# The lead of an attention-and-MLP kernel: projection tiles in groups of four, two begun on either half of the array's rows

## The chip, the cores and the metric

The kernel runs on one core of a Trainium2 chip. The metric is the device time of one execution in microseconds (us). Engines are named as in the profile: PE is TensorE (matmuls), PEld its weight loads, DVE is VectorE, ACT is ScalarE, POOL is GpSimd, SP is SyncE, which here issues all the DMAs (its queue is SPq). "L305" is line 305 of the kernel.

## What is computed

```
xn  = layernorm(x)                       # x: 2048 rows, 512 wide, f32
qkv = xn @ wqkv                          # 32 heads of 16
p   = softmax(q @ k.T * 16 ** -0.5)      # per head, 2048 x 2048
s   = (p @ v) @ wo
h   = relu(xn @ w1 + b1) ** 2            # 1792 wide
out = x + s * silu(h @ w2 + b2)
```

## The kernel before

**Halves of the array.** Every f32 operand of a projection is split into a high and a low part, and a product takes three matmuls (high by high, high by low, low by high). Most matmuls use 64 of the 128 rows, rows 0 to 63 (lane 0) or 64 to 127 (lane 1), and one of each lane can run at the same time. PE takes its instructions strictly in the written order, so the order says which two stand side by side.

**Three kinds of small work.** A max (max_mm, L305 with its reduction on DVE, L313) takes 128 x 512 scores of one head and keeps their row maximum; there are 2048 of them, 1024 per lane, in three rotating PSUM banks pm. After 64 maxes of a unit u (4 heads by 512 queries) the shift is worked out on DVE and sent through DRAM into rows of the tile qe. An exp (exp_mm, L1283, then ACT at L1289) is a score block whose exponential goes to a tile pt; its matmul writes one of three banks se. A PV step (L379) multiplies four pt tiles with v into the bank po.

**The full tiles.** After the layernorm 16 projection tiles of 128 x 512 are made with all 128 rows (q_tile, L991, 12 matmuls each), among the transposes of the layernorm and behind them. They make k and q of the first heads and most of v. Their results go to DRAM (k_d, q_d, v_d) and come back as ka (keys) and qm (queries for the maxes).

**The lead.** Then come 31 projection tiles in halves (lead_halves, L1040, 12 matmuls on lane 0 and 12 on lane 1 into one bank), with maxes in between. Lane 0 takes tile after tile; lane 1 does the same tiles 23 places later (`far = [None] * (15 + LAG)`). Before lane 1 may touch a bank, a dependency makes it wait for a later max of lane 0. At the start the list far is empty but for a few maxes, and at the end what is left in far runs beside eight maxes of lane 0. Each tile ends in q_end: ACT copies the bank to raw (L1020, two buffers), POOL splits it into hl (L82 and L83, three buffers), and SP stores hl (q_d or k_d). Beside the tiles stand, by a counter b, loads and stores for later: the transposed input to DRAM (xn_d, 1 MB each), the keys of the next heads, v, the queries qe.

**The loop.** After it, blocks ("slots") of one key block each: 512 slots with exps, maxes, matmuls of the MLP (L207 in halves, L239 in blocks of both lanes) and a PV step two slots behind. Slots 0 and 1 carry four exps and four maxes each and, by pump(6), the last projection tile, made with all 128 rows (L991 into pd). Slots 2 and 3 have no MLP matmuls. Slot 4 begins the MLP: it needs the first 256 columns of the input, xc, in four DMAs by quarters of the contraction, and the first weights w1s, which come as ex and are split by POOL. A planner (long_slots, ahead_m) chooses between two shapes of a slot pair by the number of maxes done so far.

PE, and in the first part ACT, DVE and POOL, run in the order of the program text; SP's order in the lead is left to the scheduler.

## Time and profile before

| what | us |
|---|---|
| median of 3 runs (1638.95 to 1640.37) | 1639.32 |
| the profiled execution | 1642.99 |
| its span from first to last instruction | 1641.1 |
| PE busy / DVE busy / ACT busy / POOL busy | 1621.3 / 1350.6 / 1181.7 / 516.4 |
| first matmul of the lead | 64.48 |
| first matmul of slot 2 | 189.81 |

Times inside the trace count from the start of the span. The mean granted TensorE clock over the span is 0.996. In rows of the timeline the columns are start, length, engine, line, operation, output and inputs, and in brackets the idle time just before and what ended it. In rows of windows each engine's busy time is followed by the number of its instructions, and then by the granted clock.

### The profile page before, as it was taken

What the parts mean: (1) busy time and instruction counts of PE and PEld (TensorE: products, weight loads), DVE (VectorE), ACT (ScalarE), POOL (GpSimd) and SP (SyncE); (2) the same over time, 40 slices, a digit from 0 to 9 for tenths busy, and PEclk for the clock granted to TensorE, in tenths of its full rate; (3) what the DMA queues carried; (4) which work ended last, traced back from release to release, by engine and by line L of the source; (5) the groups of instructions that cost most, each with busy time, mean ns of one, the idle gap of its engine ahead of it and who ended that gap; (6) DMA issues with size and microseconds to landing.
All of it is one profiled execution on the core that took longest, in us unless ns stands there. A gap on an engine that the chain in (4) does not pass through costs nothing.

```text
span 1641.1 us, 35386 instructions
## 1 busy us (share of the span) xinstructions
PE 1621.3 (99%) x13627; PEld 979.2 (60%) x13627; DVE 1350.6 (82%) x2335; ACT 1181.7 (72%) x2339; POOL 516.4 (31%) x541
## 2 busy tenths in 40 slices
PE   7999999999999999999999999999999999999998
PEld 6799666556656655565566556645665565454455
DVE  6399988887788888888888888888888888888843
ACT  6221477778878877787777777877877777777785
POOL 5335567513211321222123103311331133213224
PEclk9899999999999999999999999999999999999999
DMA  8596555426232522342333423343341442415444
GB/s 304 158 270 222 180 177 163 130 54 170 86 87 83 162 72 81 102 128 70 93 99 111 114 71 111 95 107 82 112 121 50 105 142 62 105 48 171 122 147 143
DMA packets 150465, 201.44 MB, mean 123 GB/s; under 512 B 50008, under 2 KB 67416, under 8 KB 148760
## 3 DMA queue, kind: packets, MB, share of 16 engines
q1 hardware_dynamic: 150296, 199.17, 41.6%
q8 instruction: 108, 1.77, 0.5%
q14 instruction: 61, 0.50, 0.1%
HBM read 144.84 MB, written 53.99 MB: 121 GB/s over the span
## 4 chain that ended last, share of the span: by engine, by line
PE 94%; DVE 2%; issue 2%; DMA 1%; POOL 0%; SPq 0%; ACT 0%; DVEq 0%
PE po L379 30%; PE pm_t L305 17%; PE pd_t L239 17%; PE se L1283 15%; PE pd_t L207 5%; PE se L1040 3%; PE pd_t L787 2%; DVE mx L313 2%; PE pd_t L1040 1%; PE po L1040 1%; PE se L991 1%; DMA ka<-k_d 1%; PE pm_t L1283 0%; DMA xt<-in_A_x_dram 0%; POOL wr_t L944 0%
## 5 line engine op out<-in xcount | busy, mean ns | idle before, releaser
L313 DVE TENSOR_REDUCE mx<-pm_t 128x1 f32<-128x512 f32 x2048 | 1267.9, 683 | 208.7 <-PE pm_t L305 123.1
L1289 ACT ACTIVATE pt<-se 128x512 f32<-128x512 f32 x1738 | 924.0, 615 | 227.3 <-PE se L1283 156.5
L305 PE MATMUL pm_t<-ka,qm 64*128 64x512 f32 x2048 | 784.5, 418 | 4.2 <-DVE mx L313 2.4
L1283 PE MATMUL se<-qe,ka 64*128 64x512 f32 x2009 | 735.0, 413 | 0.4 <-DMA qe<-sh_d 0.2
L379 PE MATMUL po<-pt,v 128*32 128x512 f32 x3554 | 526.6, 602 | 0.0
L305 PEld LDWEIGHTS pm_t<-ka,qm 64*128 64x128 f32 x2048 | 360.6, 185 | 219.5 <-DVE mx L313 205.2
L1283 PEld LDWEIGHTS se<-qe,ka 64*128 64x128 f32 x2009 | 350.5, 184 | 103.1 <-ACT pt L1289 61.8
L239 PEld LDWEIGHTS pd_t<-xc,w1s 64*128 64x128 f32 x2352 | 295.7, 187 | 47.3 <-issue 45.3
L239 PE MATMUL pd_t<-xc,w1s 64*128 64x256 f32 x2352 | 322.0, 286 | 0.0
L239 PE MATMUL pd_t<-w2t,hT 64*128 64x512 f32 x936 | 253.2, 406 | 0.0
L379 PE MATMUL po<-ex,v 128*32 128x512 f32 x542 | 226.5, 602 | 0.0
L1289 ACT ACTIVATE ex<-se 128x512 f32<-128x512 f32 x271 | 163.4, 616 | 42.1 <-PE se L1283 30.2
L239 PEld LDWEIGHTS pd_t<-w2t,hT 64*128 64x128 f32 x936 | 159.5, 184 | 48.5 <-issue 40.2
L379 PEld LDWEIGHTS po<-pt,v 128*32 128x32 f32 x3554 | 88.2, 108 | 154.3 <-issue 141.1
L558 POOL TENSOR_TENSOR r<-r 128x512 f32<-128x512 f32 x49 | 50.9, 1039 | 331.9 <-ACT r L555 331.9
L577 POOL TENSOR_TENSOR u<-u,b_t 128x512 f32<-128x512 f32 x16 | 20.7, 1296 | 365.0 <-ACT u L576 365.0
L207 PE MATMUL pd_t<-w2t,hT 64*128 64x512 f32 x408 | 106.1, 392 | 0.0
L207 PEld LDWEIGHTS pd_t<-w2t,hT 64*128 64x128 f32 x408 | 72.5, 184 | 9.6 <-DVE mx L313 0.7
L787 PE MATMUL pd_t<-wot,oc 64*128 64x512 f32 x267 | 76.9, 406 | 0.0
L417 POOL TENSOR_TENSOR ot<-ot,hl 128x512 f32<-128x512 f32 x31 | 39.8, 1284 | 109.1 <-DMA hl<-r_d 80.9
L83 POOL TENSOR_TENSOR hT<-r,hT 128x512 fp32r<-128x512 f32 x56 | 72.2, 1289 | 4.7
L1040 PE MATMUL se<-xT,wr_t 64*128 64x512 f32 x336 | 71.4, 390 | 0.0
(133 smaller groups left out, 1213.4 us busy)
## 6 DMA issues: line engine op xcount, KB each, us to landing
w1s<-w_d SPq DMA_DIRECT2D x196, 256.0 KB
k_d<-hl SPq DMA_DIRECT2D x32, 256.0 KB
xn_d<-xT SPq DMA_DIRECT2D x8, 1024.0 KB
q_d<-hl SPq DMA_DIRECT2D x16, 512.0 KB
qm<-q_d SPq DMA_DIRECT2D x128, 64.0 KB
qe<-q_d SPq DMA_DIRECT2D x128, 64.0 KB
ka<-k_d SPq DMA_DIRECT2D x32, 256.0 KB
hl<-r_d SPq DMA_DIRECT2D x31, 256.0 KB
```

Source lines behind the costliest of these rows:

```text
L83: (lo or nc.gpsimd).tensor_tensor(dst[1], raw, dst[0].bitcast(F32), op=ALU.subtract)
L207: mm = nc.tensor.matmul(out_, lh(r), rh(r), start=first_ and lane == 0, stop=last_ and lane == 1, skip_group_check=True,)
L239: mm = nc.tensor.matmul(out_, lh(r), rh(r), start=first_ and lane == 0, stop=last_ and lane == 1, skip_group_check=True,)
L305: nc.tensor.matmul(ps, qms[u][p][64 * j : 64 * j + 64, qb * P : (qb + 1) * P], kas[qd, p][64 * j : 64 * j + 64, kc * 512 : (kc + 1) * 512] ...
L313: return nc.vector.tensor_reduce(mxs[u][:, c, kc : kc + 1], ps, axis=AX.X, op=ALU.max)
L379: nc.tensor.matmul(po[32 * j : 32 * j + 32, :], vs[qd][:, (4 * kb + j) * VW : (4 * kb + j) * VW + 32], pts[j], start=(kb == 0), stop=(kb = ...
L417: nc.gpsimd.tensor_tensor(ot, ot, hl[:, 1].bitcast(F32), op=ALU.mult)
L558: nc.gpsimd.tensor_tensor(r, r, r, op=ALU.mult)
L787: inst = nc.tensor.matmul(ps[lane], oc[r, a, n, ts_], wot[r, b, n], start=m == 0 and (lane == 0 or wide), stop=m == kos and (lane == 1 or ...
L1040: inst = nc.tensor.matmul(out_, lh(r), rh(r), start=first_ and lane == 0, stop=last_ and lane == 1, skip_group_check=True,)
L1283: nc.tensor.matmul(se, kas[qd, j // 2][b : b + 64, kb * P : (kb + 1) * P], qes[u][j // 2][b : b + 64, :], start=True, stop=True,)
L1289: return nc.scalar.activation(pts[j], se, AF.Exp, scale=0.25)
```

## The change

**The lead** is now 32 tiles in eight groups of four; each group is two streams that are emitted in turn, one operation of lane 0, one of lane 1. In a group lane 0 begins tiles 0 and 2 and then finishes tiles 1 and 3; lane 1 begins 1 and 3 and finishes 0 and 2. Tiles 0 and 1 are in banks se, tile 2 in pd, tile 3 in po. LEAD_AT says after which matmuls of a stream a max stands: 11 in each stream of 48 matmuls, 10 in the first group.

**The last tile** is the fourth of the last group and no longer stands in slots 0 and 1. The eight exps of slots 0 and 1 stand in the last group, after the sixth of every twelve matmuls of a stream, all eight in one bank se that the group takes for them. The loop begins at slot 2; slots 0 and 1 are gone.

**DMAs.** SP's order in the lead is now that of the program text. The first keys and queries are loaded by halves (four loads of ka, four of qm, and again). The events by b stand at the start of every twelve matmuls of lane 0; memsets of ka move into the events b = 2 and 3, those of qm and qe behind the full tiles.

The core of the diff:

```diff
+LEAD_AT = (
+    (3, 8, 12, 17, 22, 26, 31, 36, 40, 45, 48),
+    (1, 5, 10, 14, 19, 24, 28, 33, 38, 42, 47),
+)
...
-        def lead_halves(kind, m, c):
-            ps = q_bank()
+        def lead_halves(kind, m, c, ps, lane0):
...
-                    start=first_ and lane == 0, stop=last_ and lane == 1,
+                    start=first_ and lane == lane0, stop=last_ and lane != lane0,
...
-        for n in range(8):
-            load_k(0, n)
-        qms[0] = load_q(0, "qm")
...
-        rest += [
-            ("qk", m, c) + ((True,) if (m, c) == (7, 3) else ())
-            for c in range(4) for m in (1, 5, 2, 6, 3, 7)
-        ]
+        first.enter_context(tc.manual_schedule(engines={mybir.EngineType.SP}))
+        qms[0] = []
+        for p in range(2):
+            for n in range(4):
+                load_k(0, 4 * p + n)
+            load_q_pair(0, "qm", p, qms[0])
+        rest += [("qk", m, c) for c in range(4) for m in (1, 5, 2, 6, 3, 7)]
...
-        far = [None] * (15 + LAG)
-
-        def step(near):
-            for mine in near:
-                if mine is not None:
-                    mine()
-                if far and far[0] is not None:
-                    far[0]()
-                del far[:1]
-
-        while len(rest) > 1:
...
-            (low, high), behind = lead_halves(*rest.pop(0))
-            low[6:6] = [lambda: max_mm(0)] * (1 + b % 2)
-            low.append(lambda behind=behind: behind(max_mm(0)))
-            high[4:4] = [lambda: max_mm(1)]
-            high[9:9] = [lambda: max_mm(1)]
-            if b % 2 == 0:
-                high.append(lambda: max_mm(1))
...
-        while far:
-            step([lambda: max_mm(0)] + [None] * 2)
...
+        def lead_group(g):
+            items = [rest.pop(0) for _ in range(4)]
+            pools_ = [(pe, "se"), (pe, "se"), (pd, "pd_t"), (pv, "po")]
+            parts = [
+                lead_halves(*item, pool.tile([P, 512], F32, name=name), n % 2)
+                for n, (item, (pool, name)) in enumerate(zip(items, pools_))
+            ]
+            last = g == groups - 1
+            se = pe.tile([P, 512], F32, name="se") if last else None
+            streams = []
+            for lane in range(2):
+                own, other = parts[lane::2], parts[1 - lane :: 2]
+                mms = own[0][0] + own[1][0] + other[0][1] + other[1][1]
+                at = LEAD_AT[lane][: 10 if g == 0 else 11]
...
+                for i, mm in enumerate(mms):
+                    if lane == 0 and i % 12 == 0:
+                        ops.append(lambda b=4 * g + i // 12, mm=mm: [event(b), mm()])
+                    else:
+                        ops.append(mm)
+                    if i + 1 in at:
...
+                        ops.append(m)
+                    if last and i % 12 == 5:
+                        kb, j = divmod(2 * (i // 12) + lane, 4)
+                        ops.append(
+                            lambda kb=kb, j=j: exp_mm(kb, j, pts.setdefault(kb, {}), False, se)
+                        )
...
+            for pair in zip(*streams):
+                for op in pair:
+                    op()
...
-        for st_ in range(NU * 16):
+        assert not rest
+        qs.close()
+        for st_ in range(2, NU * 16):
             if st_ < done:
                 continue
             begin(st_)
-            if st_ < 2:
-                slot(st_, [], None, 6)
-                shift_due()
-                continue
```

**On PE, at the end of the lead and in front of slot 2** (L991 and L1040 are projection matmuls of before, L1026 of the change; L305 and L308 maxes, L1283 and L1205 exps) the last tile stood between maxes and exps:

```order
L1283 MATMUL se<-qe_735,ka_205 128x512
L991 MATMUL pd_t<-xT_188,wr_t 128x512 x6
L305 MATMUL pm_t<-ka_205,qm_203 128x512
L1283 MATMUL se<-qe_734,ka_204 128x512
L305 MATMUL pm_t<-ka_205,qm_203 128x512
L1283 MATMUL se<-qe_735,ka_205 128x512
```

In the last group of the change the exps stand in pairs, one of each lane, at most two matmuls apart; the fourth pair stands like this, with pd and po the tiles that are being finished:

```order
L1026 MATMUL po<-xT_188,wr_t 128x512
L1205 MATMUL se<-qe_735,ka_205 128x512
L308 MATMUL pm_t<-ka_205,qm_203 128x512
L1026 MATMUL po<-xT_188,wr_t 128x512
L1205 MATMUL se<-qe_735,ka_205 128x512
```

Both exps of a pair write the same bank se.

**On SP, around the first loads of the MLP** (ex is the raw first weight, xc the input's first columns, k_d_64 and q_d_60 the last stores of the projections) the last q_d store stood ahead of ex and xc, and the last two k_d stores a dozen DMAs behind them:

```order
L964 DMA q_d_60<-hl 256x1x512
L451 DMA ex_2519<-in_B_w_dram 128x4x128
L493 DMA xc<-xn_d 128x2x256 x4
L451 DMA ex_2520<-in_B_w_dram 128x4x128
L451 DMA ex_2521<-in_B_w_dram 128x4x128
```

Now three stores stand between ex and xc:

```order
L454 DMA ex_2513<-in_B_w_dram 128x4x128
L970 DMA k_d_64<-hl 128x512 x2
L967 DMA q_d_60<-hl 256x1x512
L496 DMA xc<-xn_d 128x2x256 x4
L454 DMA ex_2514<-in_B_w_dram 128x4x128
L454 DMA ex_2515<-in_B_w_dram 128x4x128
```

The stores wait for POOL's split of the last two tiles, and xc has moved behind them.

More of the change, by code (lines that the diff above doesn't have):

```diff
@@ L32 @@
 SHIFT = 8
-LAG = 8
 NVT = 7
@@ L1059, in lead_halves @@
             return [
-                [lambda mm=mm, lane=lane: emit(mm, lane, lane and mm is mms[0]) for mm in mms]
-                for lane in range(2)
-            ], behind
+                [lambda mm=mm, lane=lane: emit(mm, lane, lane != lane0 and mm is mms[0]) for mm in mms]
+                for lane in (lane0, 1 - lane0)
+            ] + [behind]
         xts = {}
@@ L1237 @@
                 load_q_pair(b // 8, "qe", b % 2, qes.setdefault(b // 8, []))
-            if after_v is None and lead[1] == NT:
+            if after_v is None and lead[1] == NT and not any(
+                kind == "v" or m % 4 == 0 for kind, m, _ in rest
+            ) and b % 4 == 0:
                 after_v = b
```

121 lines of the change are left out of this document (55 added, 66 removed).

## The prediction

> **What bounds the kernel now.** I begin with the page: the busy time of the engines and the chain that ended last.
>
> ```profile
> PE 1621.3 (99%) x13627; PEld 979.2 (60%) x13627; DVE 1350.6 (82%) x2335; ACT 1181.7 (72%) x2339; POOL 516.4 (31%) x541
> PE 94%; DVE 2%; issue 2%; DMA 1%; POOL 0%; SPq 0%; ACT 0%; DVEq 0%
> ```
>
> PE is the bound: 94% of the chain is PE. Its instructions stand in a fixed order, so a microsecond that PE saves in the lead is saved at the end, unless a later wait takes it back. A busy PE is not a full PE, though: with one lane at work it counts as busy too. So next I read PE by stretches (length, busy and count, granted clock, DMA share, GB/s).
>
> ```profile
> 61.17:64.58 3.41, 3.41 (x16) 1.00 1.07 183
> 64.58:68.00 3.42, 2.50 (x13) 1.00 1.03 184
> 68.00:71.41 3.41, 3.41 (x13) 0.50 0.93 304
> 71.41:74.82 3.41, 3.41 (x11) 0.50 0.49 189
> 74.82:78.24 3.42, 3.42 (x18) 0.50 0.00 0
> 78.24:81.65 3.41, 3.41 (x32) 1.00 0.16 57
> 180.64:184.05 3.41, 3.17 (x16) 1.00 0.55 183
> ```
>
> At full clock and on both lanes 3.4 us hold 32 half-array matmuls (78.24). The first stretch of the lead holds 13; after it the granted clock is 0.50 until a stretch with 18 has passed. At the end of the lead a stretch with 16 did not lower it. So here the clock falls after about 3.4 us with 13 half matmuls or fewer, and does not with 16.
>
> Then the timeline of PE at both ends of the lead, and the first row of slot 4 that needs xc:
>
> ```profile
> 64.48 0.96 PE L1040 MATMUL pd_t<-wa_t,xT 64*128 64x512 f32 x3
> 66.36 0.47 PE L305 MATMUL pm_t<-ka,qm 64*128 64x512 f32 x1 [0.92 <-DMA ka<-k_d]
> ...
> 189.81 0.39 PE L305 MATMUL pm_t<-ka,qm 64*128 64x512 f32 x1
> ...
> 196.17 0.40 PE L207 MATMUL pd_t<-xc,w1s 64*128 64x256 f32 x2
> ...
> 197.72 1.06 PE L379 MATMUL po<-pt,v 128*32 128x512 f32 x8
> ```
>
> The lead with slots 0 and 1 takes 64.48 to 189.81, **125.3 us**. Call the start of slot 2 T: the first matmul on xc is at T + 6.4, and the PV step that closes slot 4 at T + 7.9. The pace of the middle is read from ACT's copies of finished tiles:
>
> ```profile
> 79.66 0.60 ACT L1000 ACTIVATE vt<-pd_t 128x512 f32<-128x512 f32 x1 [12.96 <-issue]
> ...
> 144.23 0.60 ACT L1020 ACTIVATE raw<-se 128x512 f32<-128x512 f32 x1 [2.89 <-PE se L1040]
> ...
> 157.68 0.60 ACT L1020 ACTIVATE raw<-se 128x512 f32<-128x512 f32 x1 [2.89 <-PE se L1040]
> ...
> 174.66 0.60 ACT L1020 ACTIVATE raw<-se 128x512 f32<-128x512 f32 x1 [2.65 <-PE se L1040]
> ```
>
> From 144.23 to 157.68 four tiles take 13.45 us; each has 12 matmuls and 2.5 maxes per lane, so these are 58 steps of both lanes: **0.232 us a step**.
>
> **The lead, in steps.** By its table the changed lead has 48 + 10 steps in the first group, 48 + 11 in six groups and 48 + 11 + 4 (exps) in the last: 475, at 0.232 us **110.2 us**. The same work at full pairing would have been 477 steps before; the other 14.6 us there are one lane idle at both ends, the halved clock, the 0.92 us wait for ka, and waits in slots 0 and 1.
>
> The start: do the first keys come in time? Before, they were issued behind a weight load:
>
> ```profile
> 51.21 1.17 SPq L967 DMA_DIRECT2D k_d<-hl  x2
> ...
> 55.69 0.39 SPq L952 DMA_DIRECT2D wv<-in_A_wqkv_dram  x1
> 56.20 0.43 SPq L135 DMA_DIRECT2D ka<-k_d  x1
> ```
>
> Now four ka and four qm loads follow these two stores, and that weight load and some xn_d stores come later. With the landing times below (3.1 us, and 1 us per 256 KB queued) they are there by about 62.5, ahead of 64.48. So PE goes from full tiles to full pairs, and the clock stays up.
>
> **Added wait 1: the exps of a pair share one bank.** The second exp's matmul waits until ACT has read the first; behind it the whole of PE waits, since its order is fixed, and with PE the maxes.
>
> ```profile
> 183.36 0.47 PE L1283 MATMUL se<-qe,ka 64*128 64x512 f32 x1
> ...
> 183.86 1.15 ACT L1289 ACTIVATE pt<-se 128x512 f32<-128x512 f32 x2 [0.25 <-DMA qm<-q_d]
> ```
>
> Matmul to ACT is 0.5 us, ACT 0.6 (1.15 for two), and about 0.1 back: 1.2 us against one step of 0.23, a hole of 0.95, four times: **3.8 us**. The bounds are 2.3 (four times ACT alone) and 6.2 (a raw copy of 0.6 ahead of each exp on ACT). I take 3.8, since only the first and last pair have raw copies near them.
>
> **Other waits of the lead.** DVE gets 22 maxes in a group of 59 steps, 13.7 us.
>
> ```profile
> L313 DVE TENSOR_REDUCE mx<-pm_t 128x1 f32<-128x512 f32 x177 | 110.2, 684 | 18.5 <-PE pm_t L305 15.9 <-PE se L1283 0.9 <-PE pd_t L1040 0.8
> ```
>
> At 110.2 / 177 = 0.62 us each that is 13.7: DVE is just as full as PE, where before it had 5 maxes in 3.36 us. Small waits for a free bank must follow a shift, which adds four small DVE instructions. Before, the 28 tiles between the copies at 79.66 and 174.66 lost 0.8 us against their 406 steps; I take **1.3**, bounds 0 and 5.
>
> So slot 2 begins at 64.5 + 110.2 + 3.8 + 1.3 = 179.8, **10.0 us earlier**.
>
> **Added wait 2: xc behind the last stores.** This is the step that gives most of it back. POOL's time for a tile, and SP's rows at the end of the lead before, with the two arrivals of ex:
>
> ```profile
> 135.92 0.62 POOL L82 TENSOR_SCALAR hl<-raw 128x512 fp32r<-128x512 f32 x1 [3.70 <-DMA q_d<-hl]
> ...
> 137.88 0.62 POOL L82 TENSOR_SCALAR hl<-raw 128x512 fp32r<-128x512 f32 x1
> ```
>
> ```profile
> 185.72 0.53 SPq L964 DMA_DIRECT2D q_d<-hl  x1
> 189.34 0.39 SPq L451 DMA_DIRECT2D ex<-in_B_w_dram  x1
> 189.79 2.03 SPq L493 DMA_DIRECT2D xc<-xn_d  x4
> 191.86 3.35 SPq L451 DMA_DIRECT2D ex<-in_B_w_dram  x3
> ```
>
> ```profile
> 192.41 0.41 POOL L82 TENSOR_SCALAR w1s<-ex 128x256 fp32r<-128x256 f32 x1 [0.40 <-DMA ex<-in_B_w_dram]
> ...
> 197.23 0.41 POOL L82 TENSOR_SCALAR w1s<-ex 128x256 fp32r<-128x256 f32 x1 [2.41 <-DMA ex<-in_B_w_dram]
> ```
>
> Before, xc was issued from T on. Now SP must first pass the stores of the two tiles that end with the lead, and these wait for POOL: the matmuls end at T, ACT's first copy at T + 0.7, and POOL needs 1.96 us a tile, so the last is done at T + 4.7. The q_d store goes out, and xc at T + 5.3 to T + 6.8. An ex took 3.07 us from issue to POOL (189.34 to 192.41); the next, with four xc ahead of it, came 4.8 us later, so a 256 KB transfer takes about 0.96. The quarters of xc land at T + 8.4, 9.3, 10.3 and 11.2, or up to 1 us later behind the q_d store's 512 KB. PE wants the first at T + 6.4. With the last quarter's matmuls slot 4 closes at about T + 11.7 and not T + 7.9: **+3.8**, bounds 1.5 (each quarter alone lands in 2 us and the holes are filled by the exps between) and 5. Behind the waiting matmul stand exps, maxes and PV steps, so nothing covers it. The later weights have their slack: the second ex lands near T + 12.5, for slot 6 at about T + 15.6.
>
> **The clock again.** From T + 6.4 to T + 11.7 PE has 8 half matmuls of 512 columns and 12 of 256, worth 14 in 5.3 us, or 9 in 3.4 us. By the rows above that is below the 13 after which the clock fell. Slots at half clock hold more than the 18 after which it came back, so I count one stretch of 3.4 us at half speed: **+1.7**, bounds 0 and 5.1 (three stretches, as at 68.00). The Trainium skill, page "TensorE: Matmul & The Clock Gate", section "What's actually happening", says that the clock falls after at least one idle window of about 3.4 us. No hole here is that long, so by that rule this term is 0; the trace speaks against it, since the clock fell at 68.00 after a stretch in which PE idled 0.92 us.
>
> **The rest of the loop.** By the two orders 174 maxes are done before slot 2 and not 178. The planner then takes the narrow pair shape four times more often. In the trace a wide pair lasts 5.47 us from PV to PV, a narrow one 5.71:
>
> ```profile
> 561.12 1.93 PE L379 MATMUL po<-pt,v 128*32 128x512 f32 x16
> 566.59 0.62 PE L379 MATMUL po<-ex,v 128*32 128x512 f32 x1
> ...
> 573.15 1.07 PE L379 MATMUL po<-pt,v 128*32 128x512 f32 x8
> ...
> 578.86 1.06 PE L379 MATMUL po<-pt,v 128*32 128x512 f32 x8
> ```
>
> 4 x 0.24 is **+1.0**; otherwise the same instructions follow.
>
> **The sum.** -10.0 + 3.8 + 1.7 + 1.0 = **-3.5 us**. The profiled execution took 1642.99, so it would take 1639.5; on the median of 1639.32 that is **1635.8**. About 0.2% (3.3 us) is what a measurement of this kernel can tell from no change; the forecast lies on that edge.
>
> **Rivals.**
> - *The clock holds in slot 4* (the rule of the clock as stated above, or quarters of xc that come evenly): the term 1.7 goes, **1634.1**. For it: the end of the lead before, with 16, kept its clock.
> - *xc comes nearly in time* (slots 2 and 3 slower, transfers faster): 1.5 in place of 3.8 and no clock loss, **1631.8**. Against it: the last issue alone is at T + 6.8, after PE wants the first quarter.
> - *The clock stays down for three stretches*, as at 68.00: 3.4 more, **1639.2**. Against it: those stretches had one lane.
> - *Slower: the stores hold up the ring of hl.* Three hl buffers, four tiles a group: if a store needs longer than 8.3 us from POOL's end to its landing, 4/3 x (lag + 1.96) exceeds the 13.7 us of a group, and PE waits for banks.
>
> ```profile
> 108.09 1.30 POOL L83 TENSOR_TENSOR hl<-raw,hl 128x512 fp32r<-128x512 f32 x1
> ...
> 119.03 0.62 POOL L82 TENSOR_SCALAR hl<-raw 128x512 fp32r<-128x512 f32 x1 [2.83 <-DMA q_d<-hl]
> ```
>
> This hl was done at 109.4 and free at 119.0, a lag of 9.6: a group would take 15.4, 1.7 more; with the wait of 3.70 at 135.92 some 3.8 more. Over groups 2 to 5, 7 to 15 us; at 9 the time is **1644.8**. Against it: before met the same lag with the same need per tile and lost little, and more xn_d stores now go out early.
>
> **Chances.** Forecast 0.40, clock holds 0.22, xc nearly in time 0.14, three stretches 0.12, slower ring 0.12. The forecast is split by its edge (0.21 faster, 0.19 same), the second is nearly all faster (0.20), the third faster (0.14), the fourth same, the fifth 0.10 slower. So faster 0.55, same 0.35, slower 0.10. The range runs from 1631.0, below the third case, to 1641.5, above the fourth; about 0.05 lies below and 0.12 above.
>
> **What would show it.** Right, if the profile after has: no wait and no 0.50 clock near 64 to 78; a copy rhythm of 13.7 us per group; four holes of about 1 us in front of the second exps in the last 15 us of the lead; slot 2 near 180; PE waiting for xc in slot 4 until T + 11, and the clock at 0.50 for about 3.4 us behind it. Wrong, if slot 2 comes after 183 with waits of POOL for hl, or if slot 4 closes before T + 9.

## The result, and the profile after

| | before | after |
|---|---|---|
| median of four executions each (us) | 1639.84 (1638.95 to 1640.44) | 1650.68 (1649.37 to 1653.13) |
| ratio, 95% interval | | 1.0062 (1.0049 to 1.0076) |
| the profiled execution / its span | 1642.99 / 1641.1 | 1653.13 / 1651.3 |
| first matmul of the lead / of slot 2 | 64.48 / 189.81 | 64.82 / 190.26 |
| PV step that closes slot 2, 4, 5 | 192.14, 197.72, 200.59 | 192.59, 203.87, 208.85 |

The change is **slower by 0.62%**, 10.8 us, where 3.5 us faster was forecast. On the base: of the 86 plain executions of the kernel before that ran beside the experiments, 75 show a mean granted clock of 0.999 or 1.000 (median 1639.74) and 11 one of 0.996 or 0.997 (median 1643.97), and both profiled executions of it are of the second kind.

The page of the change first: PE's share and its place in the chain.

```profile
PE 1618.6 (98%) x13639; PEld 966.7 (59%) x13639; DVE 1351.5 (82%) x2335; ACT 1182.0 (72%) x2339; POOL 515.9 (31%) x541
PE 93%; DVE 3%; DMA 2%; ACT 1%; POOL 0%; SPq 0%; issue 0%; DVEq 0%; POOLq 0%; ACTq 0%
```

PE's share of the chain has gone from 94% to 93%, and DMA's from 1% to 2%, on a longer span: PE is busy for 2.7 us less and waits more. What it waits for between 60 and 230 us (total, times, longest):

```profile
PE pd_t L1026 <- ACT raw L1007: 8.2, 1, 8.2
PE pd_t L210 <- DMA xc<-xn_d: 3.8, 2, 3.2
PE se L1205 <- ACT pt L1211: 2.1, 4, 0.7
```

One wait of 8.2 us in the lead is new and was not in my sum; the other two are the two added waits that I had counted. ACT's copies of finished tiles show where the first one lies:

```profile
102.44 1.09 ACT L1007 ACTIVATE raw<-se 128x512 f32<-128x512 f32 x2 [9.36 <-PE se L1026]
...
116.33 1.09 ACT L1007 ACTIVATE raw<-se 128x512 f32<-128x512 f32 x2 [8.62 <-PE se L1026]
...
130.17 0.60 ACT L1007 ACTIVATE raw<-se 128x512 f32<-128x512 f32 x1 [8.57 <-PE se L1026]
136.54 0.60 ACT L1007 ACTIVATE raw<-se 128x512 f32<-128x512 f32 x1 [5.77 <-POOL hl L86]
138.47 0.60 ACT L1007 ACTIVATE raw<-po 128x512 f32<-128x512 f32 x1 [1.33 <-POOL hl L86]
144.93 0.60 ACT L1007 ACTIVATE raw<-pd_t 128x512 f32<-128x512 f32 x1 [5.86 <-POOL hl L86]
154.71 1.09 ACT L1007 ACTIVATE raw<-se 128x512 f32<-128x512 f32 x2 [9.19 <-PE se L1026]
...
168.61 1.08 ACT L1007 ACTIVATE raw<-se 128x512 f32<-128x512 f32 x2 [8.64 <-PE se L1026]
```

A group takes 13.9 us from copy to copy (102.44 to 116.33, 154.71 to 168.61), as forecast but for 0.2. One group, 130.17 to 154.71, takes 24.5: **10.6 us lost in one place**, where ACT waits for POOL. The chain of waits says what POOL waited for:

```profile
122.37 5.98 DMA sh_d<-sq
...
131.45 2.92 DMA k_d<-hl
...
137.78 4.97 DMA k_d<-hl
...
143.63 1.27 POOL hl L86
...
144.93 0.61 ACT raw L1007
145.54 0.04 issue
145.58 0.79 PE pd_t L1026
```

Read from below: PE's bank pd was free when ACT had copied it, ACT needed a raw that POOL had to split, POOL needed an hl, and hl came free when its k_d store had landed. That store was late because of what SP, in program order, had ahead of it. It went out at 137.11, 14.2 us behind its split: for the first 5.4 of these SP stood waiting for sh_d to land, and for the other 8.7 it issued what stood in between (four loads of rows, another k_d and a q_d store, six loads of queries and keys, an xn_d store). SP's queue around it, and the two POOL rows of the tile concerned (its split ends at 121.64 + 1.29 = 122.93, and its buffer is taken again at 142.93):

```profile
114.65 3.68 SPq L1244 DMA_DIRECT2D b_t<-in_B_b_dram  x1
118.37 1.96 SPq L1247 DMA_DIRECT2D b_t<-in_B_b_dram  x1
...
121.73 0.54 SPq L1252 DMA_DIRECT2D xn_d<-xT  x1
122.37 0.65 SPq L353 DMA_DIRECT2D sh_d<-sq  x1
128.37 2.07 SPq L373 DMA_DIRECT2D qe<-sh_d  x4
...
130.97 0.85 SPq L970 DMA_DIRECT2D k_d<-hl  x2
...
136.46 0.55 SPq L1252 DMA_DIRECT2D xn_d<-xT  x1
137.11 1.65 SPq L970 DMA_DIRECT2D k_d<-hl  x2
```

```profile
121.64 1.29 POOL L86 TENSOR_TENSOR hl<-raw,hl 128x512 fp32r<-128x512 f32 x1
...
142.93 0.62 POOL L85 TENSOR_SCALAR hl<-raw 128x512 fp32r<-128x512 f32 x1 [4.49 <-DMA k_d<-hl]
```

The clock by stretches, behind the stop and in slots 4 and 5 (length, busy and count of PE, PEld, DVE, ACT and POOL, granted clock, DMA share, GB/s):

```profile
136.90:140.31 3.41, 0.50 (x6) 0.06 (x2) 1.58 (x3) 0.84 (x2) 1.46 (x2) 1.00 0.97 321
140.31:143.73 3.42, 0.00 (x0) 0.00 (x0) 0.00 (x0) 0.00 (x0) 0.71 (x2) 0.50 1.08 409
...
147.14:150.55 3.41, 3.41 (x20) 2.66 (x18) 2.08 (x3) 0.00 (x0) 1.55 (x2) 0.50 0.68 253
...
194.93:198.34 3.41, 1.86 (x12) 0.46 (x12) 2.36 (x4) 1.89 (x4) 2.23 (x4) 1.00 0.92 304
198.34:201.75 3.41, 1.13 (x9) 0.82 (x9) 0.69 (x1) 0.01 (x1) 0.00 (x0) 1.00 0.92 285
201.75:205.17 3.42, 3.40 (x19) 1.62 (x17) 1.38 (x2) 1.78 (x3) 1.16 (x3) 0.50 1.14 290
205.17:208.58 3.41, 3.41 (x23) 2.75 (x20) 1.98 (x3) 1.47 (x3) 3.16 (x6) 0.50 0.55 187
```

So the clock is at half for 10.24 us from 140.31, inside the stop (137.40 to 145.58), and for 6.83 us from slot 4 on. The drop of before at 68.00 is gone, as forecast. Slot 4 itself, on SP and on PE:

```profile
194.72 0.53 SPq L967 DMA_DIRECT2D q_d<-hl  x1
195.29 2.97 SPq L496 DMA_DIRECT2D xc<-xn_d  x4
```

```profile
199.98 0.35 PE L210 MATMUL pd_t<-xc,w1s 64*128 64x256 f32 x1 [3.18 <-DMA xc<-xn_d]
...
203.87 1.94 PE L382 MATMUL po<-pt,v 128*32 128x512 f32 x8
...
208.85 1.06 PE L382 MATMUL po<-pt,v 128*32 128x512 f32 x8
```

With T = 190.26, xc was issued from T + 5.0 (forecast T + 5.3), and slot 4 closed at T + 13.6 (forecast T + 11.7). From the PV step of slot 2 to that of slot 5 the change takes 16.26 us, before 8.45: **7.8 us lost**. Below I call this the loss up to slot 5. In the expectations the same row (208.85) is named the step of slot 6; that is a slip of mine in counting.

The ledger of the two profiled executions, as the distance of the change's PV steps from those of before: +0.45 at slot 2 (-10 was forecast), +7.8 more up to slot 5, then -0.9 at slot 8 and -0.9 at slot 24 (waits of before that have gone), +1.4 at slot 41 (a max waits 1.09 for DVE), and +1.25 between slots 124 and 135, where four pairs are narrow instead of wide. These make +9.1; the other 1.1 of the +10.2 by which the spans differ comes in steps of about 0.3 (slots 10, 26, 74 and 80).

### The profile page after: what moved, and what is told of

It is laid out like the page before. It is cut to its first block, busy times and chain, and to the rows that moved or that the text cites. A ratio compares the mean times of both kernels' runs of the same rounds, so it can differ in the third digit from the quotient of the medians.

```text
span 1651.3 us, 35404 instructions
## 1 busy us (share of the span) xinstructions
PE 1618.6 (98%) x13639; PEld 966.7 (59%) x13639; DVE 1351.5 (82%) x2335; ACT 1182.0 (72%) x2339; POOL 515.9 (31%) x541
## 4 chain that ended last, share of the span: by engine, by line
PE 93%; DVE 3%; DMA 2%; ACT 1%; POOL 0%; SPq 0%; issue 0%; DVEq 0%; POOLq 0%; ACTq 0%
PE po L382 30%; PE pd_t L242 17%; PE pm_t L308 16%; PE se L1205 15%; PE pd_t L210 6%; PE se L986 2%; PE pd_t L790 2%; PE se L1026 2%; DVE mx L316 2%; PE pd_t L1026 1%; PE po L1026 1%; DMA sh_d<-sq 1%; DMA k_d<-hl 0%; PE pm_t L1205 0%; PE pm_t L1082 0%; DMA xc<-xn_d 0%
## 5 line engine op out<-in xcount | busy, mean ns | idle before, releaser
L308 PE MATMUL pm_t<-ka,qm 64*128 64x512 f32 x2048 | 795.6, 417 | 2.8 <-DVE mx L316 2.5
L1205 PE MATMUL se<-qe,ka 64*128 64x512 f32 x2009 | 735.0, 413 | 2.6 <-ACT pt L1211 2.1
L308 PEld LDWEIGHTS pm_t<-ka,qm 64*128 64x128 f32 x2048 | 362.4, 185 | 219.2 <-DVE mx L316 204.1
L1205 PEld LDWEIGHTS se<-qe,ka 64*128 64x128 f32 x2009 | 350.9, 184 | 103.3 <-ACT pt L1211 68.4
L382 PE MATMUL po<-ex,v 128*32 128x512 f32 x538 | 218.3, 602 | 0.0
L558 ACT ACTIVATE r<-pd_t,b_t 128x256 f32<-128x256 f32 x98 | 42.1, 496 | 30.8 <-PE pd_t L242 30.8
```

The source lines that it names most:

```text
L308: nc.tensor.matmul(ps, qms[u][p][64 * j : 64 * j + 64, qb * P : (qb + 1) * P], kas[qd, p][64 * j : 64 * j + 64, kc * 512 : (kc + 1) * 512] ...
L382: nc.tensor.matmul(po[32 * j : 32 * j + 32, :], vs[qd][:, (4 * kb + j) * VW : (4 * kb + j) * VW + 32], pts[j], start=(kb == 0), stop=(kb = ...
L558: nc.scalar.activation(r[:, i], ps[:, i * CW : (i + 1) * CW], AF.Relu, bias=b1_t[:, fo : fo + 1])
L1205: nc.tensor.matmul(se, kas[qd, j // 2][b : b + 64, kb * P : (kb + 1) * P], qes[u][j // 2][b : b + 64, :], start=True, stop=True,)
```

## The experiments

**Theory A** for the stop: SP's order. Whatever stands ahead of the stores on SP (a load that waits for another landing, slow issues) makes them late, and late stores empty the ring of hl. **Theory B**: bytes. The stores go out but lie behind megabytes in the transfers. For slots 2 to 5: SP's order of xc behind stores that wait for POOL, against a clock that falls there anyway. All edits are to the change unless another kernel is named.

### The shift's rows three events later

```diff
-                if u < 2:
-                    back()
+                if u < 2:
+                    rows_due.append((now[0] + 3, back))
```

(event(b) runs what is due.)

> The change, with the four loads of the shift's rows (qe<-sh_d) of units 0 and 1 issued three events of the lead later than the shift's store, so that the k_d and q_d stores of the group stand ahead of them on SP. Theory A (SP's order: it stood 5.3 us waiting for the landing of sh_d, and the k_d store of a tile that POOL had finished at 119.0 went out at 130.97 behind it, so hl, raw and the banks filled up): the stop of 8.2 us at 137 to 145 and the halved clock behind it (140 to 150) are gone, slot 2 begins at 180 to 182 instead of 190.7, and the time is 1640 to 1642 against the change's 1650.7. Theory B (bytes: with 1 MB xn_d stores and keys among them the 16 DMA engines are behind, whatever the order on SP): the stores still land 9 us or more after POOL, the stop stays at 5 us or more, slot 2 at 187 to 191, the time 1647 to 1651.

Measured: 1645.75 us, ratio to before 1.0029 (1.0012 to 1.0047), 4.9 us below the change. The stop shrank from 8.2 to 2.8 us; the clock still fell behind it, for 6.83 us. Between the two theories: SP had become free of the rows but not of the slow b_t loads. The same tile on POOL (split done at 121.98, buffer taken again at 136.60, 14.6 us later and not 20.0):

```profile
120.68 1.30 POOL L86 TENSOR_TENSOR hl<-raw,hl 128x512 fp32r<-128x512 f32 x1
...
136.60 0.62 POOL L85 TENSOR_SCALAR hl<-raw 128x512 fp32r<-128x512 f32 x1 [3.25 <-DMA k_d<-hl]
```

### Rows and biases later

The edit above, and the two b_t loads at k == 13 instead of k == 4.

> The change, with two things moved out of the way of the stores on SP: the shift's rows (as in the run with the rows alone, where the stop of PE fell from 8.2 to 2.8 us and slot 2 came 4.9 us earlier against the first copies), and the two slow loads b_t (SP spent 5.4 us on issuing them at 113.5 to 118.9), nine events later. Same bytes in the lead. Theory A (order on SP): the k_d store behind POOL's end at 118.0 now goes out by 119 and not at 123.7, the stop of PE and the half clock at 138 to 145 are gone, slot 2 comes 10 us earlier than in the change (against the first copies), and the time is 1640 to 1642. Theory B (bytes): the stop stays at 2 us or more, because the 1 MB xn_d stores stand ahead of the k_d stores in the transfers; 1643 to 1646.

Measured: 1642.33, ratio 1.0013 (1.0004 to 1.0023), 8.4 below the change. The bytes of the lead are the same, only their order on SP has changed, and the stop is gone with its half clock: in the waits of PE between 60 and 230 us the line for raw is missing.

```profile
PE pd_t L210 <- DMA xc<-xn_d: 3.1, 1, 3.1
PE se L1206 <- ACT pt L1212: 2.1, 4, 0.7
```

The profiled execution (1640.14) is the fastest of the ten. In it slot 2 begins at 180.20 and its PV step stands at 182.54, 9.6 us earlier than before's. Theory A holds for the stop; B alone would have left it. A store 11.3 us behind its split, the latest of this kernel, cost nothing:

```profile
122.32 1.30 POOL L86 TENSOR_TENSOR hl<-raw,hl 128x512 fp32r<-128x512 f32 x1
...
134.90 0.62 POOL L85 TENSOR_SCALAR hl<-raw 128x512 fp32r<-128x512 f32 x1 [1.35 <-DMA k_d<-hl]
```

### The xn_d stores spread over eight groups

```diff
-            if b % 2 and b < 16:
-                c, i = divmod(b // 2, 2)
+            if b % 4 == 1:
+                c, i = divmod(b // 4, 2)
```

> The change, with SP's order otherwise kept, but the eight xn_d stores of 1 MB one in each group of four tiles instead of two in each of the first four groups. Theory A (order): the rows' loads still hold SP until sh_d has landed, the b_t loads still cost their 5.4 us; less lies ahead of sh_d, so the stop of PE is 3 to 6 us instead of 8.2; slot 2 comes 2 to 6 us earlier, the time is 1644 to 1648. Theory B (bytes): with half the xn_d bytes in the groups where it stood, the stop is under 1 us, the clock stays up, slot 2 comes 10 us earlier: 1640 to 1641.

Measured: 1649.00, ratio 1.0055 (1.0041 to 1.0070), 1.7 below the change; the stop is 5.3 us, inside the 3 to 6 of theory A and far from B's. Bytes do play a part: of the 2.9 us by which the table's buffer is free earlier, 1.2 are SP's (the store goes out 13.0 us behind its split and not 14.2) and 1.7 the store's own way (4.1 us from issue to the free buffer and not 5.8, with no 1 MB store just ahead of it). The time is above A's 1644 to 1648, and its interval overlaps the change's; a clock at half for 6.83 us stayed behind the stop.

```profile
121.79 1.30 POOL L86 TENSOR_TENSOR hl<-raw,hl 128x512 fp32r<-128x512 f32 x1
...
140.18 0.62 POOL L85 TENSOR_SCALAR hl<-raw 128x512 fp32r<-128x512 f32 x1 [2.24 <-DMA k_d<-hl]
```

Set side by side, for the third tile of the group that ends at 120 (end of its split, the issue of its k_d store on SP, the next use of its buffer, the lateness with its two parts, and the longest wait of PE for raw):

| kernel | split done | store issued | buffer taken | late | split to issue | issue to buffer | stop | late - stop |
|---|---|---|---|---|---|---|---|---|
| the change | 122.93 | 137.11 | 142.93 | 20.0 | 14.2 | 5.8 | 8.2 | 11.8 |
| xn_d spread | 123.09 | 136.07 | 140.18 | 17.1 | 13.0 | 4.1 | 5.3 | 11.8 |
| rows later | 121.98 | 130.06 | 136.60 | 14.6 | 8.1 | 6.5 | 2.8 | 11.8 |
| rows and biases later | 123.62 | 128.31 | 134.90 | 11.3 | 4.7 | 6.6 | 0 | |

Theory B would show in the way from issue to free buffer, theory A in the way from split to issue. The first stays at 4 to 7 us; the second falls from 14.2 to 4.7, and the stop with it.

The stop is the lateness less 11.8 us, to a tenth. In the change's rows the 11.8 reads so: PE wanted pd at 145.58 - 8.18 = 137.40; from the free buffer to the free bank it takes 145.58 - 142.93 = 2.65; so a buffer free by 134.75, 11.8 behind 122.93, would cost nothing. For the change alone that is the same subtraction; that the other kernels give the same 11.8, and that 11.3 late cost nothing, is the test.

### Four hl buffers

```diff
-        hlp = right(qs, "hlp", 3)
+        hlp = right(qs, "hlp", 4)
```

> The change with four hl buffers instead of three, so that a whole group's tiles fit. Theory A and B both say that the ring passes the lateness on; a fourth buffer takes up one tile's worth of it, 3.4 us. Worked out from the trace of the change: POOL could take the first tile of the next group at 134.5, when the late k_d store has landed, instead of the fourth tile of the old group; the third raw copy then waits until 136.5 instead of 138.5 and the fourth until 138.5 instead of 144.9, so the stop of PE shrinks from 8.2 to 1 to 4 us, slot 2 begins at 182 to 186, and the time is 1641 to 1646. If the ring were not what stops PE (the banks wait for something else, as the two raw buffers or ACT), the stop stays at 8 us and the time at 1650.

Measured: 1643.53, ratio 1.0026 (1.0017 to 1.0036), 7.2 below the change. The stop is 1.6 us and the clock stays up in the lead. The order on SP is the change's own, and the first k_d store is as late as ever: its buffer is taken again at 134.58 (134.51 in the change). So the ring is what carries the lateness to PE, and one more buffer covers nearly all of it.

### SP left to the scheduler

```diff
-        first.enter_context(tc.manual_schedule(engines={mybir.EngineType.SP}))
```

> The change, with SP's order in the lead left to the scheduler as before. The scheduler's order differs in the loads of keys (one half set of them ahead), in the two b_t loads (ahead of the k_d stores of the third group, before v) and in the keys; but the store of sh_d and its loads stand again ahead of the k_d store of the fourth group. If the fixed order by itself is the fault, the stop goes and the time is 1640 to 1642. By theory A (whatever stands ahead of the stores, by any hand): a stop of 3 to 6 us stays, since the rows' loads still wait for sh_d ahead of the stores, and the b_t loads no longer add to it: 1644 to 1649.

Measured: 1641.94, ratio 1.0014 (1.0005 to 1.0023), 8.7 below the change. There is no stop: the line for raw is missing from PE's waits between 60 and 230 us.

```profile
PE pd_t L210 <- DMA xc<-xn_d: 3.7, 2, 3.1
PE se L1204 <- ACT pt L1210: 2.1, 4, 0.7
```

My expectation of 3 to 6 us failed: the rows' loads do still hold SP for 3.6 us ahead of a k_d store, which goes out 6.9 us behind its split (12.0 in the change), but the b_t loads are issued by 102.1, and the next two stores follow at once, without queries, keys and xn_d among them. The buffer of the table's tile is free again within 10.0 us, below 11.8. So theory A holds as a sum, not as one culprit, and the **fixed order on SP** is the part of the change that brought the stop.

### The exps of a pair six matmuls apart

```diff
-                    if last and i % 12 == 5:
+                    if last and i % 12 == (5, 11)[lane]:
```

> The change with the exps of lane 1 in the last group six matmuls later than those of lane 0, so that the two exps of a pair do not meet in their shared bank. My term for the shared bank was 3.8 us; the trace of the change shows 2.1 us of waiting in four waits, and the last group takes 17.0 us where the others take 13.9. If the bank is the whole of it: the four waits are gone, the last group takes about 15.0, and the time is 2 us below the change's, 1648.5. If ACT is the limit in that group instead (its raw copies and exps in turn): no change, 1650.5.

Measured: 1649.60, ratio 1.0062 (1.0047 to 1.0077), 1.1 below the change. Of the four waits on pt, 2.1 us, one of 0.3 is left, and the last group takes 14.6 us instead of 17.0 (from 166.54 to 181.15 in ACT's copies, 168.61 to 185.63 before the edit). The shared bank is the whole of that term. In the median the gain is not seen (the ratio is the change's own), and in this trace the clock fell once more, at 312.02 for 3.41 us.

### The last stores issued by POOL

qk_store issues the k_d and q_d stores of the last two tiles with nc.gpsimd instead of nc.sync.

> The change, with the stores of the last two projection tiles (k_d and q_d of columns 1536 to 2047) issued from POOL's queue, behind the splits that they wait for, so that on SP the four loads of xc follow the first ex directly. My theory for the second loss (xc behind stores that wait for POOL: PE waited 3.2 and 0.6 us in slot 4, and the clock was halved for 6.8 us behind it; the PV step of slot 4 stood at +6.2 against before and that of slot 6 at +8.3, where slots 2 and 3 stood at +0.45): xc is issued about 4 us earlier, PE waits less than 0.5 us for it, the clock stays at 1.00 in slots 4 to 6, and the time is 6 to 8 us below the change's, 1643 to 1645. Rival: the wait goes, but the clock falls all the same because slots 4 and 5 hold little for PE: 4 us below, 1647. Rival: xc isn't issued earlier, because it waits for the space that hl or the input leaves: no gain, 1650.

Measured: 1650.57, ratio 1.0074 (1.0059 to 1.0089), no gain. xc went out 1.3 us behind slot 2's first matmul (191.94) and not 5.0, so 3.8 us earlier against it, as expected. PE's waits for it fell to 2.0 us (0.8 the longest), and the loss up to slot 5 from 7.8 to 5.8, but PE then waited 1.0 for w1s, whose split now stood behind the DMA issues on POOL, and the clock fell for 3.41 us in slots 4 and 5 and once more at 316.50. No verdict on the mechanism.

### The last two tiles split by ACT and DVE

```diff
-            if not lead[0]:
+            if not lead[0] or (c == 3 and m in (3, 7)):
```

> The change, with the last two projection tiles split by ACT and DVE straight from PSUM (as the full tiles are) and not by ACT and POOL, so that their stores wait 2 us and not 4.7 for their split, and xc, behind them on SP, goes out earlier. In the change xc was issued at 195.3 to 198.3, slot 2 having begun at 190.7, and PE lost 5.7 us up to the PV step of slot 4 and 7.8 up to slot 6, with a clock halved for 6.8 us. If the stores' wait for POOL is the reason: xc goes out 2 to 2.5 us earlier, the loss up to slot 6 is 3.5 to 5.5, and the time is 2 to 4 us below the change's, 1646.5 to 1648.5. If the transfers' queue is (the stores' bytes and the landing), or the first pair's stores, which still wait for POOL until 0.4 us behind the start of slot 2: within 1 us of the change, 1649.5 to 1651.

Measured: 1653.57, ratio 1.0079 (1.0064 to 1.0093), 2.9 above the change, against the expectation. The loss up to slot 5 did fall, to 4.4, but two DVE instructions more at the end of the lead made maxes wait, 2.4 us in three waits up to 230 us (0.6 in two in the change), slot 2's PV step came 1.8 later against ACT's last copies of v (105.8 us behind 89.57; in the change 104.0 behind 88.59), and the clock fell at 203.15 and again at 315.79, for 3.41 us each.

### The last stores in slot 4

Three kernels store the last two tiles in slots 3 or 4, behind xc; they differ in where the split halves lie meanwhile: in two pt tiles and the hl of the normalisation; in ot, one pt tile and that hl; in the second v tile (idle until slot 48) and that hl.

```diff
-            qk_store(m, c, hl)
+            waiting.append((4, store))    # the last two tiles
```

> The change, with the k_d and q_d stores of the last two projection tiles in slot 4, from buffers that stay (the split is POOL's as before), so that xc goes out on SP right behind the stores of the pair before them. Theory order (xc stood behind stores that wait for POOL): xc is issued from T + 0.5 on, T being the start of slot 2, the loss up to the PV step of slot 6 falls from 7.8 to 1 to 3 us, and the time is 5 to 7 us below the change's: 1643.5 to 1645.5. Theory bytes (1 MB of the earlier pair's stores and the ex loads still lie ahead of xc in the transfers): the loss falls to 5 or 6, the time 1648 to 1649.

> The change, with the last two tiles' stores behind xc as in the run that put them in slot 4, but with one borrowed pt tile instead of two (the high half of one tile lies in ot) and stored one slot earlier, so that no exp waits for a pt tile (ACT waited 2.9 us there, which cost PE 1.4). Theory order (xc stood behind stores waiting for POOL): PE waits under 0.5 us for xc, the loss from the first PV step of the loop to that of slot 6, 7.8 us in the change and 4.2 with the two borrowed tiles, falls to 1 to 3, the clock stays at 1.00 there, and the time is 1644 to 1646 (5 to 6.5 below the change). Rival (slots 2 to 5 hold too little for the clock, whatever PE waits for): the clock still falls there and the loss stays at 3.5 to 5, the time at 1647 to 1649.5.

> The change, with the last two tiles' stores in slot 4 behind xc, and no pt tile borrowed: one tile's halves lie in the second v tile, which is idle until slot 48, the other's in the hl of the normalisation. Both earlier runs of this kind made exps wait for pt tiles (ACT 2.9 and 6.2 us). Theory order: the loss from the first PV step to that of slot 6 (7.8 us in the change) falls to 1 to 3, with PE waiting 1 us or less for xc and the clock at 1.00, the time 1643.5 to 1646. Rival (the clock falls in slots 4 to 6 all the same): loss 3.5 to 5, time 1647 to 1649.

Measured: 1649.33 (ratio 1.0056, 1.0041 to 1.0071), 1653.37 (1.0075, 1.0062 to 1.0089) and 1648.97 (1.0057, 1.0043 to 1.0071). The first two are spoilt by the edit: with pt tiles on loan, exps waited on ACT for one, 2.9 and 6.2 us; the losses up to slot 5 are 4.2 and 5.9, and in the second the clock fell once more, at 314.78.

```profile
203.72 1.58 ACT L1233 ACTIVATE pt<-se 128x512 f32<-128x512 f32 x3 [6.19 <-DMA k_d<-pt]
```

The third borrows none. In it xc was issued at 191.05, 1.2 us behind slot 2's first matmul, and PE waited 1.2 us for it in three waits, 0.5 the longest. The loss up to slot 5 is 4.4 and not 7.8, but the clock fell all the same, behind a stretch in which PE was busy for 2.51 of 3.41 us:

```profile
193.88:197.30 3.42, 2.63 (x19) 0.83 (x15) 2.99 (x5) 2.51 (x5) 1.43 (x3) 1.00 0.96 294
197.30:200.71 3.41, 2.51 (x21) 1.51 (x23) 1.38 (x2) 1.41 (x3) 1.17 (x3) 1.00 0.89 243
200.71:204.12 3.41, 3.41 (x18) 1.66 (x20) 1.52 (x3) 0.98 (x2) 3.05 (x6) 0.50 0.97 352
```

But in the first of the three runs the clock did not fall in slots 2 to 5 at all, with PE busy for even less of the thinnest stretch, and 4.2 us were lost all the same:

```profile
200.87:204.28 3.41, 2.04 (x22) 1.49 (x18) 2.00 (x4) 0.70 (x2) 3.16 (x7) 1.00 1.05 379
```

So SP's order is worth 3.4 of the 7.8 us. The rival does not explain the rest: it is there with the clock down and with the clock up. Of the 4.4 us that are left in the third run, PE's waits for xc are 1.2 and the half clock is about 1.7 (half of 3.41, an estimate); the other 1.5 lie in no wait that the trace names. In the median the edit brought 1.7 us, which is inside the intervals.

### The kernel before once more

> The kernel before, unchanged, for one more profile. Its first profile has the clock at 0.50 from 68.00 to 78.24 and took 1642.99, but its plain runs stand at 1639.3 to 1640.5 and nearly all show a mean clock of 0.999 or 1.000, not 0.996. If the halved clock in the lead was an accident of that one execution: this profile has no stretch at 0.50 before the end, slot 2 begins 3 to 4 us earlier than 189.81 (about 186, apart from the start), and the execution takes 1639 to 1640. Then 3.5 of the 10 us that my prediction let the lead win were not there to be won. If it belongs to the kernel: the same stretch at 0.50 and 1642 to 1643.

Measured: 1644.77, span 1643.0, mean clock 0.996. My expectation failed: the second profiled execution has the same wait for ka and the same 10.24 us at half clock (69.68 to 79.92).

```profile
67.76 0.46 PE L305 MATMUL pm_t<-ka,qm 64*128 64x512 f32 x1 [1.11 <-DMA ka<-k_d]
```

```profile
66.27:69.68 3.41, 2.30 (x13) 1.62 (x12) 1.38 (x3) 1.61 (x3) 3.34 (x2) 1.00 1.00 166
69.68:73.10 3.42, 3.42 (x12) 2.72 (x10) 2.41 (x5) 0.00 (x0) 0.26 (x1) 0.50 0.97 330
```

So it is no accident of one execution: it comes in both profiled ones and, by their clocks, in 11 of 86 plain ones. 10.24 us at half clock lower a mean over 1641 us by 0.003, which is the step from the 75 executions (0.999 or 1.000) to the 11 (0.996 or 0.997), and the 11 are 4.2 us slower; that their clock fell in the same place is inferred, since plain executions leave no trace. The profile of before had thus been taken of an execution that is some 4 us slower than the one that the median measures.

### Everything together

Four versions, each with rows and biases later, four hl buffers and the exps apart: with xn_d spread and the split by ACT and DVE; with xn_d spread and the last stores in slot 4 from two pt tiles; with the stores from ot and one pt tile; with the stores from the v tile (the last two with xn_d as in the change).

> All together: rows and biases later, xn_d spread, four hl buffers, the last two tiles split by ACT and DVE, and the exps of a pair apart. If my ledger of the change holds, the terms add: the stop and the half clock of the lead -10.6, the exps -2.1, xc -2 to -4, against the change's 1650.5: 1634 to 1636, which is 4 to 6 us below the kernel before, and what the lead was worth. If the clock falls in slot 4 as before and something else is late instead, 1637 to 1640.

> As the run with everything, but with the last two tiles split by ACT and POOL again (the split by ACT and DVE cost 2 to 3 us of waiting for DVE at the end of the lead) and stored in slot 4. Against that run's 1636.9: 1 to 2 from the DVE waits, 2 to 4 from xc if the order of the stores is what holds it: 1632 to 1634. If bytes hold xc: 1635 to 1636.

> Rows and biases later, four hl buffers, exps apart, and the last stores as in the clean run; xn_d as in the change, since its last MB stood near xc when it was spread. Theory order: slot 2 as early as with everything together (about 92 us behind the first pair of copies, against 104 in the change), the loss up to slot 6 under 3 us: 1631 to 1634. Rival (the clock falls in slot 4 all the same, for 3.4 to 6.8 us): 1635 to 1638, no better than the two runs with everything.

> Rows and biases later, four hl buffers, exps apart, and the last two stores in slot 4 from the second v tile. Theory order: the lead as in the other runs with everything (slot 2 about 13 us earlier in the trace than before's 189.81), the loss up to slot 6 at 1 to 3 us: 1632 to 1634.5. Rival (the clock): 1635.5 to 1637.5.

Measured, against before: 1636.87, ratio 0.9980 (0.9971 to 0.9989); 1637.54, 0.9980 (0.9971 to 0.9989); 1638.39, 0.9990 (0.9980 to 0.9999); 1637.17, 0.9986 (0.9977 to 0.9995). The first and second **beat the kernel before by 0.2%**, 3.6 and 2.4 us by the medians, and the change by 13 to 14. All miss the lower times that I hoped for: with slot 2's PV step 12.8 to 13.5 us earlier than before's, they lose 5.1 to 6.6 up to slot 5, with the clock at half there for 3.41 or 6.83 us. In the first of them PE still waits 2.7 us for xc.

## Why the prediction was wrong, point by point

- **The lead in steps: right.** 475 steps at 0.232 us gave slot 2 at 179.8. That is 115.3 us from 64.5. With rows and biases later, and nothing else, the lead runs from 65.50 to 180.20, 114.7 us. That the two lie within 0.6 is partly luck: the exps took 1.7 less than their term, and what is left over the steps and the exps is 2.4 and not 1.3. The start without a wait for ka, the pairing and the 13.7 us of a group all came (13.9 measured).
- **Exps of a pair in one bank: right in kind, too large.** 2.1 us against 3.8, just below my lower bound of 2.3: each wait was 0.5 and not 0.95. The second exp did start 1.1 us behind the first (174.93 behind 173.85, where I took 1.2), but the matmuls between them covered 0.4 to 0.6 of that, and I had counted one step of 0.23.
- **The ring of hl: the step that failed.** I gave "the stores hold up the ring of hl" a chance of 0.12 and argued against it with "before met the same lag with the same need per tile and lost little". The mechanism and even its price (7 to 15 us over the sum; 10.6 measured) were in the rivals. What I missed is that the lag was not the same: I took before's 9.6 us as a property of the transfers, but in the change's runs it is made by what stands ahead of a store on SP (14.2 of the 20.0 us, against 4.7 of 11.3 with rows and biases later), and the change fixed SP's order. I read the new order of SP at the end of the lead, and not in the middle, where sh_d, its four loads, two slow loads and an xn_d store stand ahead of the k_d stores. The lag there became 20.0 us. My threshold of 8.3 us was for a lag that lasts; a single late store is forgiven up to 11.8. Before, too, sh_d and its loads stood ahead of stores (sh_d at 125.61, the next q_d store at 132.59) and POOL waited 3.70 for a buffer, but PE did not wait: the rows alone are not enough.
- **The clock behind the stop: not in the sum.** Of the 10.6 us the stop is 8.2; the other 2.4 are about half of the 5 us at half clock that follow it (145.58 to 150.55). The Trainium skill, page "TensorE: Matmul & The Clock Gate", section "What's actually happening", says that the clock falls after at least one idle window of about 3.4 us; here the trace comes close to that, since PE was busy for 0.50 us between 136.90 and 140.31 and had stood still for 2.9 when it fell. In slot 4 of the run with the v tile it fell after a stretch with PE busy for 2.51 of 3.41 us, which that rule does not foresee. A later section of that page, "A second HAM failure mode: psum-queue depth-cycling", tells of another kernel (bf16, cycling through PSUM banks) whose clock swings because PE idles in short gaps, without a bound; PE's gaps were short here too (0.5 at most), but no run here swings like that.
- **What the clock follows: nearer to the prediction's count.** The prediction counted half matmuls (13 fell, 16 held). Counted in matmuls of 512 columns (one of 256 as half, one that an edge cuts by its share, both lanes together), the stretches of 3.41 us in all 18 traces (laid out from the first fall of each, from 62 us to 8 us before the end, without those that hold full-array matmuls) read so: behind all 8144 with 12.6 or more the clock was full, behind all 51 with 11.2 or less it was half, and of the 12 between 7 were followed by half clock. So it fell behind 10.5 in the run with the v tile (PE busy for 2.51 us) and held behind 13.7 in the run with two pt tiles on loan (busy for 2.04): the busy time does not decide.
- **xc behind the last stores, and the clock: right in kind, too small.** The forecast was 3.8 + 1.7 = 5.5; it was 7.8. PE's wait for xc came out at the 3.8 of the sum, in a wait of 3.2 and one of 0.6; what was mis-sized is the clock, at half for two stretches and not one, so 3.4 and not 1.7 (at half their length, as in the sum). I took it that a slot at half clock holds more than the 18 after which the clock had come back; the first of the two stretches (201.75) holds 19 by the row, but seven of them have 256 columns and its edges cut others, and by the count above it holds 12.3. That leaves 0.6, which no row names. The rival "the clock holds in slot 4" did not come true in the change; it did in the run with two pt tiles on loan, which lost 4.2 us there even so.
- **The narrow pairs: right.** Four of them, 1.25 us against 1.0. Two waits of before that vanished (-1.8) and a wait for DVE at slot 41 (+1.4) I had not looked for; with the small steps of the ledger (+1.1) they add 0.7.
- **The base: wrong, and it was visible.** I took the sum against the profiled execution and shifted it onto the median. But 3.7 us between 1642.99 and 1639.32 were about the price of the half clock at 68.00, a loss that most plain executions don't have. What the change saves there is saved in the profile and in few plain executions. The run with rows and biases later shows the two apart: its span is 2.7 us below before's (1638.4 against 1641.1, close to my -3.5), its median 1.85 us above before's 1640.48. Only about half of that difference is before's half clock (1642.99 against a median of 1640.48); the other half is that the profiled execution of this run, 1640.14, lies 2.2 below its own median. Without the stop my forecast would have been met against the profile and, at 1642.33, missed against the median.

What stays open: what decides the clock between 11.2 and 12.6 matmuls a stretch (the five that held have PV steps among them, and so have three of the seven followed by half clock), where the last 1.5 us up to slot 5 go, and why both profiled executions of before have the half clock at the start of the lead (its first stretches there hold 11.2 and 11.6, close to that edge).

## What to carry to other kernels

When an order is fixed by hand on the queue that issues all DMAs, list for every store what stands ahead of it in that queue, above all loads that wait for another transfer's landing, and compare its lateness with what the ring of buffers forgives; a lag seen in the old order says nothing about the new one. Where the profiled execution is slower than the median by about the price of something that it shows, ask whether the median has it at all before counting its removal as a gain. Look also at what the new order puts ahead of the first loads of the next stage: here up to slot 5 the change lost 7.8 us though its slot 2 was no earlier than before's, and the versions with slot 2 some 13 us earlier lost 5.1 to 6.6, so the loss came with the order there more than with the earlier start.

## What the runs showed of the hardware

- The stop of PE was the lateness of one store less 11.8 us (11.7 to 11.9 by the rounded waits) in all nine kernels with three buffers that had the stop: the three of the table, the run with the exps apart (19.5 late, 7.7 lost), the one with stores on POOL (19.9, 8.1), the split by ACT and DVE (19.8, 8.1) and the last stores in slot 4 (20.2, 8.4; 19.5, 7.7; 20.2, 8.3).
- Two loads of biases held SP's queue for 5.6 us (3.68 and 1.96) where they stood amid other transfers; nine events later they took 0.40 and 0.76, with the DMAs moving 54 GB/s there and 169 to 276 around the first place.
- The busy time of PE does not tell whether the clock falls: it fell after stretches with PE busy for 1.13 us (the change) and 2.51 us (last stores from the v tile), and held after 1.86 us (the change, from 194.93), 1.84 us (four hl buffers, from 136.91) and 2.04 us (last stores in slot 4). The matmuls in the stretch tell it better: full clock behind 12.6 or more of 512 columns, half behind 11.2 or fewer, in every stretch of these traces that holds no full-array matmul.
